# Two token tiles of x, each loaded in two parts of rows on two DMA queues

## The chip, the cores and the metric

The kernel runs on one core of one Trainium2 chip. The metric is the device time of one execution in microseconds. A profile of one execution goes with it: all times of day below are microseconds from the start of that execution's span. TensorE is PE in the profile (PEld for its weight loads), VectorE is DVE, ScalarE is ACT, GpSimd is POOL and SyncE is SP.

## The reference

The input x has 2048 tokens of 512 features in bf16. It is normalised without scale or shift, and two branches run on the result: a diagonal state-space layer (S5) and a SwiGLU feed-forward layer. Both are added to x.

```python
x = A_x
xn = _layernorm(x, axis=-1)
return x + _A_ref(xn, ...) + _B_ref(xn, B_w_gate, B_w_up, B_w_down)
...
g = _silu(x @ w_gate)
u = x @ w_up
return (g * u) @ w_down
...
h = Lam_bar[None, :] * h + Bu[:, t, :]
...
y = 2.0 * jnp.einsum("blp,dp->bld", hseq, Cmat).real + x * Dskip[None, None, :]
```

The hidden width of the feed-forward layer is 1376, the state size 512.

## The kernel before, in words

**Tiling.** The tokens are cut into 16 tiles of 128 and four chunks of 512. The features are cut into four blocks of 128 (index k). The hidden width of 1376 is cut into groups of 512, 512 and 352 columns (`fgroups`, L89). Everything is written out once; the engines run their instructions in the order of the program, and semaphores join them.

**The first chunk is special.** TensorE has nothing to do until tokens arrive, so the first tiles are handled with the tokens as the stationary operand. Tiles 0 and 1 of x are not normalised first. TensorE transposes the raw rows with an identity matrix (`raw_mm`, L233, matmuls at L230), VectorE adds up each row in the meantime (`sum_dve`, L222), and a small matmul takes the mean off the transposed tile in PSUM (`cT_mean`, L238). ScalarE and VectorE copy the result to SBUF (`raw_copy`, L245). Then the products with w_up follow, one feature block k at a time (`row_mm`, L712, matmuls at L487): four matmuls of 512 columns for each k, two tiles by two column groups. The products with w_gate come next, and the scale of the normalisation is put on when ScalarE reads the products (L495, L507). Tiles 2 and 3 are centred or normalised first.

**The loads at the start.** SyncE's queue carries, in this order: tile 0 of x (L123), the four rows of w_up (L117, one for each k, 256 KB each), two rows of w_gate, tile 2 of x (L131), a row of w_gate, tile 3 (L133), the last row of w_gate, the ends of both weights (L113), and tiles 4 to 7 (L141). Tile 1 of x goes on ScalarE's queue (L125), ahead of the load of ScalarE's activation table (L126). A small write of zeros by VectorE into tile 1 (L124) comes before it: the transfer overwrites those bytes and so waits for the write. GpSimd's queue carries three small rows of parameters (L140). A program assigns the transfers of SyncE and ScalarE to eight semaphores in turn, so that one is not issued before the transfer eight places earlier has landed.

**The dummies.** While the first tile is on its way, TensorE multiplies constants (`dummy`, L666, matmuls at L668): four matmuls of 512 columns and then five of 128 (L692 and L693). Their results are not used. They stand ahead of all other work in TensorE's order.

**After that** the chunks follow in a software pipeline: products with the S5 input matrix (L380), gate and up products (L455), the scan on VectorE (L422), the down products (L598) and the S5 output products (L611) accumulate in one PSUM bank for each output tile.

The lines around the change:

```python
120  ident = const.tile([128, 128], BF16, name="ident")
121  make_identity(nc, ident[:])
123  nc.sync.dma_start(out=xall[:, 0, :], in_=x_v[:, 0, :])
124  nc.vector.memset(xall[:, 1, 0:2], 0.0)
125  nc.scalar.dma_start(out=xall[:, 1, :], in_=x_v[:, 1, :])
126  nc.scalar.preload_act_table_set("silu_and_others")
127  for k in range(KD):
128      load_row(nc.sync, wu01, wu_v, k)
...
692  dummy(warm, 4, CW)
693  dummy(warm, 5, 128)
697  raw_mm(0)
```

Of the kernel before, what the change touches and what calls it, by code (L numbers as in the profile page):

```python
# [23 lines left out]
def kernel(  # L24
# [17 lines left out]
    nc = tc.nc  # L42
# [37 lines left out]
    x_v = A_x[0].rearrange("(n p) d -> p n d", p=128)  # L80
# [5 lines left out]
    xall = const.tile([128, NT, D], BF16, name="xall")  # L86
# [33 lines left out]
    ident = const.tile([128, 128], BF16, name="ident")  # L120
    make_identity(nc, ident[:])
    minus_mean = const.tile([128, 128], BF16, name="minus_mean")
    nc.sync.dma_start(out=xall[:, 0, :], in_=x_v[:, 0, :])  # L123
    nc.vector.memset(xall[:, 1, 0:2], 0.0)  # L124
    nc.scalar.dma_start(out=xall[:, 1, :], in_=x_v[:, 1, :])  # L125
    nc.scalar.preload_act_table_set("silu_and_others")  # L126
    for k in range(KD):
        load_row(nc.sync, wu01, wu_v, k)
# [97 lines left out]
    warm = pair[0][0][1]  # L226
# [439 lines left out]
    def dummy(ps, n, cols):  # L666
        for _ in range(n):
            nc.tensor.matmul(ps[:, 0:cols], lhsT=one.to_broadcast([128, 128]), rhs=one.to_broadcast([128, cols]),  # L668
                             start=True, stop=True)
# [20 lines left out]

    G, U = wg_g, wu_g
    dummy(warm, 4, CW)  # L692
    dummy(warm, 5, 128)  # L693
    nc.vector.tensor_scalar(out=minus_mean[:], in0=ident[:], scalar1=-1.0 / D, scalar2=None, op0=ALU.mult)
    for i in range(2):
        sum_dve(i, sums[:, i:i + 1])
# [208 lines left out]
```

## Time and profile before

| | |
|---|---|
| time, median of 3 runs | 178.27 us (178.15 to 178.41) |
| span of the profiled execution, first to last instruction | 175.8 us |
| median over the span | 2.5 us more |
| TensorE busy | 171.4 us |
| VectorE busy | 156.9 us |
| ScalarE busy | 102.0 us |
| GpSimd busy | 28.1 us |
| read from and written to HBM | 8.03 and 5.24 MB |

The profile records one execution. Its own time is known by its span; what lies before the first and after the last instruction is not in it, and the medians of the runs stand 2.5 us above the span. Several views of the trace are used. The chain that ended last is followed back from the last instruction, at each step to what released it. The timeline lists instructions in order of time, merged where one follows another of the same line. A view by window gives each engine's busy time, the granted TensorE clock, the share of the DMA engines' time that was used and GB/s. "Us to landing" is the time from the issue of a transfer to the semaphore that tells that all of it has arrived. An engine name with a q (SPq, ACTq) is that engine's sequencer, which issues transfers.

### The profile page before, as it was taken

The numbers are of one execution on the slowest core, as the hardware profiler recorded it, in microseconds if no ns is written. First come the engines' busy times: TensorE is split into PE (matmuls) and PEld (weight loads), VectorE is DVE, ScalarE is ACT, GpSimd is POOL, SyncE is SP. The second block draws the span as 40 slices with busy tenths as digits, with TensorE's granted clock in tenths as the row PEclk, the third lists the DMA queues.
The fourth block names the chain that finished last, engine by engine and source line by source line (L and its number), as shares of the span: only waits on it lengthen the run. The fifth ranks groups of instructions, "written<-read, shape, count | busy, mean of one in ns | idle before, by whom it ended". The sixth has DMA issues, their size and how long they took to land.

```text
span 175.8 us, 2365 instructions
## 1 busy us (share of the span) xinstructions
PE 171.4 (97%) x847; PEld 82.6 (47%) x863; DVE 156.9 (89%) x259; ACT 102.0 (58%) x188; POOL 28.1 (16%) x39
## 2 busy tenths in 40 slices
PE   8999999999999999999999999999999999999993
PEld 4544446464444444446444444446444444444542
DVE  3776999999999999999999999999999998699542
ACT  3379498793997685236598660024666653990100
POOL 5244110032000000044300000025000000522500
PEclk9999999999999999999999999999999999999999
DMA  5998929999999300047016000007200000696921
GB/s 184 344 350 83 245 48 205 285 191 300 161 218 306 112 4 0 0 38 82 2 34 119 0 0 0 0 0 87 36 15 17 0 4 0 87 175 96 117 66 60
DMA packets 34043, 17.88 MB, mean 102 GB/s; under 512 B 24896, under 2 KB 32928, under 8 KB 33984
## 3 DMA queue, kind: packets, MB, share of 16 engines
q1 hardware_dynamic: 30288, 14.22, 34.1%
q0 software_dynamic: 3456, 3.28, 14.4%
q10 hardware_dynamic: 288, 0.23, 0.4%
q8 instruction: 7, 0.11, 0.3%
q14 instruction: 4, 0.03, 0.1%
HBM read 8.03 MB, written 5.24 MB: 75 GB/s over the span
## 4 chain that ended last, share of the span: by engine, by line
PE 96%; DMA 1%; issue 1%; DVE 0%
PE ps L455 29%; PE ps L598 22%; PE ps L611 16%; PE ps L380 16%; PE ps L487 8%; PE ps L541 3%; PE ps L771 2%; DMA xall<-in_A_x_dram 1%; PE ps L230 1%; PE ps L238 0%; DVE xall L614 0%; PE ps L271 0%
## 5 line engine op out<-in xcount | busy, mean ns | idle before, releaser
L598 PE MATMUL ps<-wd_sb,guT 128*128 128x512 bf16 (+4 forms) x184 | 38.7, 366 | 0.2
L422 DVE TENSOR_TENSOR_SCAN g<-r_t,car,u 128x512 bf16<-128x512 f32 x24 | 29.1, 1264 | 0.0
L611 PE MATMUL ps<-CF,wt 128*128 128x512 bf16 (+2 forms) x134 | 28.4, 366 | 0.1
L380 PE MATMUL ps<-xnT,BT 128*128 128x512 bf16 x125 | 28.1, 379 | 0.2
L598 PEld LDWEIGHTS <-guT 128*128 128x128 bf16 (+1 forms) x187 | 17.9, 98 | 20.5
L455 PE MATMUL ps<-xnT,wu 128*128 128x512 bf16 x95 | 24.6, 379 | 0.2
L455 PE MATMUL ps<-xnT,wg 128*128 128x512 bf16 x91 | 23.9, 379 | 0.1
L618 POOL DMA_DIRECT2D out_dram<-res x12 | 10.5, 1043 | 77.3 <-ACT res L617 72.1
L469 ACT ACTIVATE guT<-ps 128x512 bf16<-128x512 f32 x30 | 18.3, 609 | 4.8 <-PE ps L455 4.5
L470 ACT CAST u<-ps 128x512 bf16<-128x512 f32 x30 | 17.9, 596 | 4.6 <-PE ps L455 4.5
L382 ACT CAST u<-ps 128x512 bf16<-128x512 f32 x32 | 17.5, 597 | 4.8 <-PE ps L380 3.3
L611 PEld LDWEIGHTS <-wt 128*128 128x128 bf16 x136 | 13.0, 98 | 14.7
L380 PEld LDWEIGHTS <-BT 128*128 128x128 bf16 x128 | 12.5, 98 | 14.8
L617 ACT CAST res<-ps 128x512 bf16<-128x512 f32 x12 | 6.8, 583 | 21.0 <-PE ps L611 21.0
L572 ACT ACTIVATE xr<-xall,nb,rstd 128x512 bf16<-128x512 bf16 x16 | 11.8, 805 | 9.1 <-DVE xall L580 4.9
L455 PEld LDWEIGHTS <-wu 128*128 128x128 bf16 x96 | 9.4, 98 | 11.3
L455 PEld LDWEIGHTS <-wg 128*128 128x128 bf16 x96 | 9.3, 98 | 10.6
L192 POOL TENSOR_TENSOR rstd<-ve,neg_half 128x1 f32<-128x1 f32 (+1 forms) x7 | 7.6, 1079 | 29.4 <-DVE ve L191 29.0
L455 PE MATMUL ps<-xnT,w_end 128*128 128x512 bf16 x48 | 10.9, 379 | 0.0
L182 DVE BATCH_NORM_STATS2 stats<-xall 128x6 f32<-128x512 bf16 x16 | 10.8, 675 | 0.0
L474 DVE TENSOR_TENSOR guT<-guT,u 128x1024 bf16<-128x1024 bf16 x15 | 10.0, 675 | 0.0
L390 DVE TENSOR_TENSOR pm<-g,c 128x2048 bf16<-128x2048 bf16 x8 | 9.8, 1220 | 0.1
(120 smaller groups left out, 207.8 us busy)
## 6 DMA issues: line engine op xcount, KB each, us to landing
out_dram<-in_A_x_dram SPq DMA_DIRECT2D x3, 512.0 KB, 5.3
out_dram<-res POOLq DMA_DIRECT2D x12, 128.0 KB, 3.1
out_dram<-xall POOLq DMA_DIRECT2D x3, 512.0 KB, 6.0
wd_sb<-in_B_w_down_dram SPq DMA_DIRECT2D x1, 1280.0 KB, 8.2
wu<-in_B_w_up_dram SPq DMA_DIRECT2D x4, 256.0 KB, 3.8
wg<-in_B_w_gate_dram SPq DMA_DIRECT2D x4, 256.0 KB, 4.8
xall<-in_A_x_dram SPq DMA_DIRECT2D x1, 1024.0 KB, 7.0
xall<-in_A_x_dram SPq DMA_DIRECT2D x1, 512.0 KB, 6.1
```

The lines of the kernel that those rows point to most:

```text
L182: nc.vector.bn_stats(out=stats[:, n, 0, :], in_=xall[:, n, :])
L380: nc.tensor.matmul(ps[:] if c else by_k(ps[:]), lhsT=BT[:, part, k, q * 128:(q + 1) * 128], rhs=xnT[:, c, k, :] if c else xnT0[:, k], star ...
L382: nc.scalar.copy(out=u_tiles[c][:, part, q, :], in_=ps[:])
L422: V.tensor_tensor_scan(out=g()[:, part, q, :], data0=r_t[:, q:q + 1].to_broadcast([128, CW]), data1=u_tiles[c][:, part, q, :], initial=ini ...
L455: nc.tensor.matmul(ps[:fs, lo:hi], lhsT=wslice(groups, fi, k), rhs=xnT[:, c, k, lo:hi], start=(k == 0), stop=(k == KD - 1))
L469: nc.scalar.activation(out=guT[:fs, fi, :], in_=psg[:fs], func=ACT.Silu)
L470: nc.scalar.copy(out=u_pair[c][:fs, fi % 2, :], in_=psu[:fs])
L487: nc.tensor.matmul(ps[:, 0:(b - a) * 128], lhsT=tokens(i, k), rhs=groups[gi][:, k, 0:(b - a) * 128], start=(k == 0), stop=(k == KD - 1))
L572: nc.scalar.activation(out=box["xr"][:], in_=xall[:, n, :], func=ACT.Identity, scale=rstd[:, n:n + 1], bias=nb[:, n:n + 1])
L598: nc.tensor.matmul(o[:], lhsT=gu_tiles[c][:fsz[fi], fi, i * 128:(i + 1) * 128], rhs=wd_sb[:fsz[fi], fi, lo:hi], start=(fi == 0), stop=False)
L611: nc.tensor.matmul(o[:], lhsT=w_tiles[c][:, part, q, i * 128:(i + 1) * 128], rhs=CF[:, part, q, lo:hi], start=False, stop=(part == 1 and q ...
L618: nc.gpsimd.dma_start(out=out_v[:, n, lo:hi], in_=res[:, lo:hi], accum_op=ALU.add)
```

## The change

Tiles 0 and 1 of x are each loaded in two parts: rows 0 to 87 by SyncE's queue, rows 88 to 127 by ScalarE's. Both queues take tile 0 first and tile 1 after it. The write of zeros is gone, and nothing holds a transfer. The dummies are four of 512 columns and three of 128.

```diff
-    nc.sync.dma_start(out=xall[:, 0, :], in_=x_v[:, 0, :])
-    nc.vector.memset(xall[:, 1, 0:2], 0.0)
-    nc.scalar.dma_start(out=xall[:, 1, :], in_=x_v[:, 1, :])
+    XS = 88
+    for i in range(2):
+        nc.sync.dma_start(out=xall[0:XS, i, :], in_=x_v[0:XS, i, :])
+        nc.scalar.dma_start(out=xall[XS:128, i, :], in_=x_v[XS:128, i, :])
     nc.scalar.preload_act_table_set("silu_and_others")
...
     dummy(warm, 4, CW)
-    dummy(warm, 5, 128)
+    dummy(warm, 3, 128)
```

## The prediction

> **What bounds the kernel now.** Start with the page's first part and its chain of work that ended last.
>
> ```profile
> PE 171.4 (97%) x847; PEld 82.6 (47%) x863; DVE 156.9 (89%) x259; ACT 102.0 (58%) x188; POOL 28.1 (16%) x39
> ...
> PE 96%; DMA 1%; issue 1%; DVE 0%
> ```
>
> TensorE is busy 97% of the span and is 96% of the chain. Only the start of the span, before TensorE has data, can be shortened by moving loads. The chain in order of time (start, length, what) shows that start.
>
> ```profile
> 0.68 0.06 issue
> 0.74 2.48 DMA xall<-in_A_x_dram
> 3.22 0.04 issue
> 3.27 0.61 PE ps L230 x4
> 3.87 0.26 PE ps L238 x2
> 4.13 0.43 PE ps L230 x4
> 4.56 0.58 PE ps L238 x4
> 5.14 4.32 PE ps L487 x20
> ```
>
> Token tile 0 of x is issued at 0.74 and lands at 0.74 + 2.48 = 3.22 us. From there on the chain is TensorE alone: transposes of tile 0 (L230), mean corrections (L238), the same for tile 1, then the up products (L487). Tile 1's landing is not in the chain. The timeline of the first microseconds shows what lies beside it (start, length, engine, line).
>
> ```profile
> 0.74 0.39 SPq L123 DMA_DIRECT2D xall<-in_A_x_dram  x1
> ...
> 0.81 0.06 DVE L124 MEMSET xall<- 128x1 uint32 x1 [0.81 <-PEq L889]
> ...
> 0.90 0.38 ACTq L125 DMA_DIRECT2D xall<-in_A_x_dram  x1
> ...
> 1.19 1.84 SPq L117 DMA_DIRECT2D wu<-in_B_w_up_dram  x4
> ...
> 1.31 1.28 ACT L126 ACT_TABLE_LOAD   x1 [1.31 <-DVE e_t L162]
> ...
> 2.02 0.15 PEld L668 LDWEIGHTS <-const-bfloat16-1.0 128*128 128x128 bf16 x1 [0.28 <-issue]
> 2.44 0.47 PEld L668 LDWEIGHTS <-const-bfloat16-1.0 128*128 128x128 bf16 x4 [0.28 <-issue]
> ...
> 3.24 0.42 DVE L222 SCALAR_TENSOR_TENSOR xnT<-xall 128x256 bf16<-128x256 bf16 x1 [1.70 <-DMA xall<-in_A_x_dram]
> 3.26 0.34 PEld L230 LDWEIGHTS <-xall 128*128 128x128 bf16 x4 [0.35 <-DMA xall<-in_A_x_dram]
> ...
> 3.73 0.13 PEld L238 LDWEIGHTS <-sums 128*128 128x128 bf16 x2
> ...
> 3.82 0.47 PEld L230 LDWEIGHTS <-xall 128*128 128x128 bf16 x4
> 4.25 0.47 PEld L238 LDWEIGHTS <-sums 128*128 128x128 bf16 x4
> ...
> 4.98 3.62 PE L487 MATMUL ps<-wu,CF 128*128 128x512 bf16 x16
> ```
>
> Read the pace out of the starts. A 512-column dummy took 2.44 - 2.02 = 0.42 us from start to start; a 128-column one (0.47 - 0.15)/3 = 0.107. The transposes at 3.82 and the corrections at 4.25 still go at 0.107. The sixteen up products go at (3.62 - 0.38)/15 = 0.216 for 512 columns. So TensorE runs at half rate into the corrections and at full rate from the first up product on; I put the change at 4.95 us. This matters most below: **work brought forward into the time before 4.95 is worth half.**
>
> **The change, part by part.** (1) Tile 0 comes as 88 rows on SyncE's queue and 40 on ScalarE's, at once, and tile 1 behind it in the same way. The packet counts of the DMA view show how it went before; q1 is SyncE's queue and q10 ScalarE's. In order, the stretches are 1.70 to 2.13, 2.13 to 2.48 and 2.48 to 2.90.
>
> ```profile
> q1 hardware_dynamic: 62, 0.06, 41.4%
> ```
>
> ```profile
> q10 hardware_dynamic: 59, 0.06, 48.4%
> q1 hardware_dynamic: 52, 0.04, 34.7%
> ```
>
> ```profile
> DMA packets 120, 0.14 MB, mean 322 GB/s; under 512 B 16, under 2 KB 92, under 8 KB 120
> ...
> q1 hardware_dynamic: 58, 0.08, 70.7%
> q10 hardware_dynamic: 62, 0.05, 35.8%
> ```
>
> Tile 0 is 128 packets of 1 KB. 62 went by 2.13, by SyncE's queue alone. Then tile 1 came in on ScalarE's queue and took 59 of the next 111 packets, so that tile 0 was not through at 2.48: of q1's 58 later packets, 120 - 92 = 28 are 2 KB packets of the weights, and about 30 are tile 0's remainder with its completion writes. The hold on tile 1 (the memset, worth 0.90 - 0.74 = 0.16 us) did not keep it out of tile 0's way. Two rows by window give the rates with one queue and with two (last column, GB/s; the 1.00 is the granted TensorE clock, which does not show the half rate).
>
> ```profile
> 1.70:2.10 0.40, 0.40 (x3) 0.12 (x2) 0.00 (x0) 0.40 (x1) 0.32 (x1) 1.00 0.40 141
> 2.10:2.50 0.40, 0.40 (x3) 0.12 (x2) 0.00 (x0) 0.40 (x1) 0.40 (x2) 1.00 0.88 305
> ```
>
> After the change both queues carry tile 0 from the start. Lower end of its landing: the 66 packets left at 2.13, alone at the rate of both queues (111 packets in 0.35 us), would be through at 2.13 + 0.21 = 2.34 instead of somewhere in 2.48 to 2.90; with the late end of that stretch, 0.5 us earlier, a landing at 2.7. Upper end: nothing gained, 3.22. Tile 1 is now issued one issue later (0.74 + 0.45 = 1.19) and meets tile 0's tail again, so I take **2.9**, near the middle. Each reader of x now waits for two transfers; I add 0.02 us for a second wait. Tile 0 is ready 0.30 us earlier.
>
> Tile 1 must follow by the time its transposes come up, 3.82 - 3.22 = 0.60 us after tile 0, at 3.5. Before, it landed at 0.90 + 2.6 = 3.5.
>
> ```profile
> xall<-in_A_x_dram ACTq DMA_DIRECT2D x1, 128.0 KB, 2.6
> ```
>
> Issued at 1.19 with the same 2.6 us it would land at 3.8, 0.3 us late, and the whole gain would be spent on waiting for it; but it too is now carried by both queues, and if it gains the 0.3 us that I give tile 0, it lands at 3.5 and is just in time. I take no stall; the other end is no gain at all, which is inside rival B's time. ScalarE issues two transfers of 0.38 us and begins its table load (1.28 us) at about 1.55 instead of 1.31; it ends at 2.8, and ScalarE's first copy comes after 3.7. That is hidden.
>
> (2) The memset goes: 0.06 us of VectorE, which waits for tile 0 from 0.94 to 3.24 anyway. Nothing.
>
> (3) Two dummies of 128 columns fewer: 2 x 0.107 = 0.21 us. The last dummy ended TensorE's queue at 2.97; now it is 2.76. With tile 0 at 2.92, five dummies would have held it up by 0.05 us. That is all this edit is worth, unless the idle time touches the pace (below).
>
> (4) What is moved: every weight load on SyncE goes one issue (0.45 us) later. The landings of the four up rows, issued at 1.19, 1.65, 2.12 and 2.60, are in two answers of the source view (min/median/max; the first for rows 0 and 1, the second for rows 2 and 3).
>
> ```profile
> DMA to landing us min/median/max: 3.0/3.3/3.6
> ```
>
> ```profile
> DMA to landing us min/median/max: 4.0/4.2/4.4
> ```
>
> They land at 4.2, 5.3, 6.1 and 7.0. They are due at 4.98 and then every 4 x 0.216 = 0.86 us: 5.84, 6.71, 7.57, so 0.5 to 0.8 us of slack. The bytes before them are the same, so the least delay is nothing, and a full issue, 0.45 us, gives 4.65, 5.75, 6.55, 7.45: still ahead of the old due times, at most level with the new ones (0.30 and later 0.15 earlier). I take no stall and keep 0.15 us for the range, all that is gained. The later loads (gate rows, tiles 2 and 3) wait for the landings of transfers eight places earlier in the order of issue, as before.
>
> **The sum.** Tile 0 at 2.92 instead of 3.22 brings the first up product from 4.98 to 4.68. The transposes before it run at the old pace. From 4.68 to 4.95 TensorE does 0.27/0.427 = 0.63 of an up product, at full rate worth 0.14 us; the last 0.03 counts whole. So 0.15 to 0.17 us less: the span goes from 175.8 to 175.65. The three times around it have a median of 178.27, 2.5 us above the span; I keep that offset: **178.1 us**. All that follows is TensorE-bound and moves with it. Here 0.2% is 0.36 us, about what a measurement of this kernel can tell from no change.
>
> The Trainium skill, TensorE: Matmul & The Clock Gate (Part 1, the clock gate), says that full rate comes after a busy window of about 3.4 us of a free-running counter, so by time and not by the number of matmuls. The trace agrees as far as one profile can: the rate changes 4.2 us after the first dummy (0.78), and by that rule bringing work forward gains half, as in the sum above.
>
> **The rivals.** A: **the whole 0.3 to 0.5 us is gained.** If the pace follows the work instead of the clock, closing TensorE's idle time between 2.97 and 3.26 brings full rate forward too. Then the gain is the landing's own: 0.30 (177.97) to 0.52 us (177.75). For it: the rate changes 0.2 us before the first up product, so a link to the work is not excluded; against it: 0.29 us of idle time is little beside the 4.2 us from the first dummy to the change.
>
> B: **the split does nothing.** If SyncE's and ScalarE's transfers only interleave, tile 0 lands at 3.2 as before; two dummies fewer only lengthen an idle time, and the time is 178.3. For it: both queues end within 0.3 us of each other today. Against it: 141 and 305 GB/s with one queue and with two. The Trainium skill, DMA: Bandwidth & Descriptors (Rules for kernel authors), takes this side: two transfers to disjoint partition halves serialize, "Use one 128-partition transfer". By that rule the time would be B's; the doubled rate in the windows speaks against it at this early moment.
>
> C: **the weights come late.** One issue (0.45 us) plus the time of one more tile at 305 GB/s (131 KB, 0.43 us) as upper end puts up row 1 at 6.17, 0.33 us after its old due time, and rows 2 and 3 by 0.3: 178.6. It decides once the delay passes the old slack of 0.55 us. The Trainium skill, DMA: Bandwidth & Descriptors (Why a DMA increments its semaphore by 16 and not by 1), says that a transfer runs on the largest number of engines up to 16 that divides its rows: 88 rows on 11, 40 on 10, the lowest-numbered ones. No trace here shows it; it would leave five engines without x and give ten of them half as much again, a reason for C.
>
> D, the slow side: **TensorE reaches full rate later.** If tile 0 still lands near 3.2, TensorE idles from 2.76, 0.5 us instead of 0.3. Should that break the warm-up, each microsecond of half rate beyond 4.95 costs 0.5 us; a whole further stretch like the one from 0.78 to 4.95 costs 2.1 us: up to 180.4. Point of decision: idle time over the 0.29 us that is known to do no harm. The trace has no such gap to price.
>
> **Chances.** Forecast 0.40 (its own range 178.0 to 178.25), A 0.25 (0.20 of it below 177.91), B 0.12, C 0.13 (0.08 above 178.63), D 0.10. So faster by over 0.2%: 0.20; within: 0.40 + 0.05 + 0.12 + 0.05 = 0.62; slower: 0.08 + 0.10 = 0.18. The range 177.6 to 178.9 takes in A's and C's ends and leaves out most of D and a little beyond both.
>
> **What would show it.** Tile 0's landing in the chain at 2.8 to 3.0 confirms step 1; 3.2 means B. The first L487 at 4.65 to 4.75, with its first start-to-start near 0.43, confirms the half rate; at 0.216 at once, it is A. A wait of PE or PEld on wu between 4.6 and 8.4 is C. Spacing of 0.43 beyond 5 us is D.

## The result and the profile after

The change made the kernel slower: 179.56 us median of 9 executions (178.59 to 181.22) against 178.18 us (177.88 to 178.89, 9 executions of the kernel before on the same chip). The ratio is 1.009, 95% interval 1.0066 to 1.0113; the medians lie 1.38 us apart. Three of the nine executions lie above 180.8 us and the other six at 178.59 to 179.65. The profiled execution of the changed kernel is one of the three: 180.86 us, span 178.7 us. In the kernel after, every line from L126 on stands one lower than before (L487 is L488).

The page's first part and its chain of work that ended last, after:

```profile
PE 174.1 (97%) x861; PEld 82.7 (46%) x861; DVE 156.9 (88%) x258; ACT 103.8 (58%) x188; POOL 28.1 (16%) x39
...
PE 96%; DMA 1%; ACT 0%; DVE 0%; issue 0%
```

TensorE is busy 2.7 us longer, though it has two dummies less to do. Of that, 1.85 us lie ahead of the first product with w_gate (9.41 us busy instead of 7.56): time went into slower matmuls there. The rest can't be read as work, because the trace of the kernel before lacks some matmul records (847 beside 863 weight loads). The chain of the first 12 us (start, length, what) and TensorE's timeline of the same stretch:

```profile
0.74 2.50 DMA xall<-in_A_x_dram
3.25 0.14 issue
3.38 0.58 PE ps L231 x4
...
4.67 0.44 PE ps L239 x3
5.11 0.02 issue
5.13 0.44 ACT CF L246 x2
5.58 0.03 issue
5.61 6.33 PE ps L488 x20
```

```profile
0.78 2.18 PE L669 MATMUL ps<-const-bfloat16-1.0 128*128 128x512 bf16 x7 [0.78 <-PEq L890]
3.38 0.58 PE L231 MATMUL ps<-ident,xall 128*128 128x128 bf16 x4 [0.42 <-DMA xall<-in_A_x_dram]
...
5.61 5.47 PE L488 MATMUL ps<-wu,CF 128*128 128x512 bf16 x16 [0.30 <-ACT CF L246]
10.91 1.03 PE L488 MATMUL ps<-wg,CF 128*128 128x512 bf16 x4
```

The last row is the first gate product. In the kernel before it is this one:

```profile
8.43 1.03 PE L487 MATMUL ps<-wg,CF 128*128 128x512 bf16 x4
```

Tile 0 lands at 0.74 + 2.50 = 3.24 us, no earlier than before (3.22). The first up product starts at 5.61 instead of 4.98, and the sixteen take 5.47 us instead of 3.62. In the starts of the single matmuls they come every 0.427 us until 9.4 us and every 0.216 us from there on: half rate lasts 4.4 us longer than before. The row names ScalarE's copy (L246) as what the first up product waited for, but the semaphore of up row 0 comes at 5.56 in the trace, last of all that it needs. The weights are late, and the view by source line says by how much (the four up rows, issued at 1.2 to 2.6 us before and 1.6 to 2.9 after; first before, then after):

```profile
DMA to landing us min/median/max: 3.0/3.8/4.4
```

```profile
L117 SPq DMA_DIRECT2D wu<-in_B_w_up_dram x4: 359/430/432, 1.6 to 2.9; - x4
...
DMA to landing us min/median/max: 4.0/5.3/5.6
```

They are issued 0.3 to 0.4 us later and take 1.0 to 1.6 us longer. The up rows land at 5.56, 7.18, 7.83 and 8.50, before at 4.19, 5.29, 6.17 and 7.00. The windows 3 to 4 and 4 to 5 us (last two columns: DMA share and GB/s), before and after:

```profile
3.00:4.00 1.00, 0.92 (x9) 0.61 (x8) 0.76 (x4) 0.00 (x0) 0.55 (x2) 1.00 1.02 343
4.00:5.00 1.00, 1.00 (x11) 0.89 (x9) 0.36 (x3) 0.27 (x1) 0.00 (x0) 1.00 1.05 296
```

```profile
3.00:4.00 1.00, 0.62 (x6) 0.50 (x7) 0.49 (x3) 0.00 (x0) 0.54 (x2) 1.00 0.88 210
4.00:5.00 1.00, 1.00 (x10) 0.94 (x9) 0.58 (x3) 0.27 (x1) 0.00 (x0) 1.00 0.72 214
```

In this pair of profiles a third of the bytes is missing while the weights should come, and the DMA engines have idle shares that they did not have before. The experiments below say how far that holds. In the first window four more profiles with the loads of before (e2, e12, e14, e15) have 258 to 329 GB/s and the splits of both tiles with five dummies or more 210 to 261, so there the split does carry less. In the second window they have 163 to 271 and 295 to 358: that shortage belongs to the profiled execution. Last, the end. SyncE's timeline has the last stores (start of the first, time until the last is issued), before and after:

```profile
168.07 5.75 SPq L615 DMA_DIRECT2D out_dram<-xall  x4
```

```profile
170.55 5.75 SPq L616 DMA_DIRECT2D out_dram<-xall  x4
```

The view of waits has what SyncE's final line waits for (total, times, longest), before and after:

```profile
SPq L900 <- DMA out_dram<-xall: 0.5, 1, 0.5
```

```profile
SPq L901 <- DMA out_dram<-xall: 1.0, 2, 0.5
```

The last store is issued by 173.82 before and by 176.30 after. From there to the end of the span (175.85 and 178.70) it is 2.03 us before and 2.40 after; after, the final line waits a second time for such a store. The program ends with SyncE waiting for the eight DMA semaphores in a fixed order. In the trace's semaphore records, the last store's semaphore is the last of the row before. After it, with 42 transfers instead of 40 on the two queues, the turn of the eight has moved on by two: the last store has the second semaphore of the row, and when it lands at 177.41 the rest of the row is still worked off, one wait per 0.062 us, until 177.79.

So the 2.85 us of these two spans divide into 0.63 until the first up product, 1.85 from there to the first gate product (8.43 to 10.91, less the 0.63), and 0.37 at the end. From the first gate product to the last store's issue both take 165.39 us. This compares a late execution of the changed kernel with a quick one of the kernel before. Of the 1.38 us between the medians the end is the same 0.37; the two parts at the start are not the median's.

### The profile page after: what moved, and what is told of

Same layout as the page of the kernel before. It is cut to its first block, busy times and chain, and to the rows that moved or that the text cites. A ratio compares the mean times of both kernels' runs of the same rounds, so it can differ in the third digit from the quotient of the medians.

```text
span 178.7 us, 2383 instructions
## 1 busy us (share of the span) xinstructions
PE 174.1 (97%) x861; PEld 82.7 (46%) x861; DVE 156.9 (88%) x258; ACT 103.8 (58%) x188; POOL 28.1 (16%) x39
## 4 chain that ended last, share of the span: by engine, by line
PE 96%; DMA 1%; ACT 0%; DVE 0%; issue 0%
PE ps L456 29%; PE ps L599 21%; PE ps L612 15%; PE ps L381 15%; PE ps L488 9%; PE ps L542 3%; PE ps L772 2%; DMA xall<-in_A_x_dram 1%; PE ps L231 1%; PE ps L239 0%; ACT CF L246 0%; DVE xall L615 0%; PE ps L272 0%
## 5 line engine op out<-in xcount | busy, mean ns | idle before, releaser
L456 PE MATMUL ps<-xnT,wg 128*128 128x512 bf16 x96 | 24.6, 379 | 0.0
```

The source lines that it names most:

```text
L456: nc.tensor.matmul(ps[:fs, lo:hi], lhsT=wslice(groups, fi, k), rhs=xnT[:, c, k, lo:hi], start=(k == 0), stop=(k == KD - 1))
```

## The experiments

Theories named in the expectations: W, rows cut 88 and 40 load the DMA engines unevenly and delay the weights; Q, two queues with four issues do so; N, each transfer ahead of the weights costs; S, it is the bytes on the second queue; P, the wait for the later part of a tile; G, too much idle time of TensorE lets one period of its clock pass at half rate; L, the row of waits at the end. Each was run beside the kernel before on the same chip. All times in us. "Onset" is when the spacing of TensorE's matmuls goes from 0.427 to 0.216 in the profiled execution.

**The parts alone: the dummies, the hold.**

```diff
e2_3dummies, from before:    -    dummy(warm, 5, 128)
                             +    dummy(warm, 3, 128)
e14_8dummies, from before:   +    dummy(warm, 8, 128)
e12_no_hold, from before:    -    nc.vector.memset(xall[:, 1, 0:2], 0.0)
```

> The loads of the kernel before, with three short dummies instead of five: the idle time ahead of tile 0 grows from 0.3 to 0.5 us. G says 179 or more. W and Q say no more than 0.2 us from before, 178.0 to 178.4, with the first up row landing at 4.2.

> The kernel before with eight short dummies instead of five, so that TensorE hardly idles ahead of tile 0. It is the one version the runs point to that could beat both. G says that no window of the kernel before fails, so there is nothing to win: ratio 0.998 to 1.001. Below 0.998 would mean that the 0.3 us of idle time costs something in the kernel before as well.

> The kernel before without the write of zeros alone: tile 1 goes out on ScalarE's queue at 0.74 instead of 0.90. N and S both expect nothing measurable, 178.1 to 178.5, with tile 0 landing up to 0.2 us later and the first up row at 4.0 to 4.3.

Measured: e2 178.31 (two of 12 executions at 179.97 and 205.47, the others up to 179.34), ratio 1.0005 [0.9982, 1.0029]; e14 178.36, 0.999 [0.9977, 1.0003]; e12 178.51, 1.0007 [0.9992, 1.0022]. Neither the dummies nor the hold alone make a difference that these intervals show. (In e2's profile tile 0 lands at 3.00, and TensorE idles for less than 0.1 us before it, so e2 hardly tests a longer idle time.) Their profiles show something else. They have the weight loads of the kernel before, but not its landings; e12, then e2 (same view as above):

```profile
DMA to landing us min/median/max: 3.0/4.5/4.8
```

```profile
DMA to landing us min/median/max: 2.9/4.5/4.7
```

In e2, e12, e14 and e15 (below) up row 1 lands at 6.02 to 6.36, in the profile of before at 5.29. That profile had caught a quick execution: its span is 175.85 us, while the median span of the kernel before in the five later sessions is 176.25 to 176.5.

**The split with other numbers of dummies.**

```diff
e1_split_5dummies, from after:  -    dummy(warm, 3, 128)
                                +    dummy(warm, 5, 128)
e7_filled, from after:          +    dummy(warm, 8, 128)
    and before the up products: +    dummy(warm, 5, 128)
```

> The split loads of the change with all five short dummies kept. Theory W (88 and 40 rows spread x unevenly over the DMA engines, so the weights come late) and theory Q (four issues on two queues at once make the weights late, however the rows are spread) both say: first up row still lands at about 5.5 us instead of 4.2, time within 0.4 us of the changed kernel, 179.2 to 179.9. Theory G (the two dummies fewer open an idle gap that delays TensorE's full rate) says: back near the kernel before, 178.0 to 178.5.

> The changed kernel with its idle times on TensorE filled: eight short dummies instead of three ahead of tile 0 and five more ahead of the first up product, 13 instead of 3. They add only useless work. G (full rate comes late because TensorE's idle times make a window of its activity fail) says: no execution over 180.2 us (the changed kernel had 3 of 9), median 178.8 to 179.2, below the changed kernel's 179.56. W and Q alone say: no faster than the changed kernel, 179.5 to 179.9.

Measured: e1 179.06 (178.59 to 179.93, 12 executions), ratio 1.0037 [1.0023, 1.005]; e7 179.19 (179.08 to 179.32, 6), 1.0055 [1.0039, 1.0072]. With TensorE kept busy no execution goes above 180, which speaks for G in the executions above 180.8; a loss of 0.4 to 0.6% stays. e1 lies between what was expected of G and of W and Q. TensorE's timeline of e1 shows the weights:

```profile
5.12 1.89 PE L488 MATMUL ps<-wu,CF 128*128 128x512 bf16 x8 [0.50 <-DMA wu<-in_B_w_up_dram]
7.38 1.89 PE L488 MATMUL ps<-wu,CF 128*128 128x512 bf16 x8 [0.37 <-DMA wu<-in_B_w_up_dram]
```

Two waits on wu, 0.87 us together, and full rate already from 4.01: the gain of an early clock is spent waiting for weights. That alone does not tell the split from the others: e4 (below), which loses nothing, waits 0.79 us for wu in two rows of the same kind.

**Other cuts of the rows.**

```diff
e3_rows96_32, from after:   -    XS = 88
                            +    XS = 96
e5_rows96_5dummies: XS = 96 and dummy(warm, 5, 128)
e9_rows112_16:      XS = 112 and dummy(warm, 5, 128)
```

> The change with the cut at row 96 instead of 88: the same four issues on the same queues, but 96 and 32 are both multiples of 16. W says the weights come back: first up row by 4.7 us, time 177.9 to 178.5. Q says nothing changes: first up row at 5.4 or later, 179.2 to 179.9. G says 179 or more too, since the dummies are as few, but with the weights on time.

> The split at row 96 with all five short dummies. Against the split at 88 with five (ratio 1.0037) it changes the spread of rows alone. W (the uneven spread of 88 and 40 rows makes the weights late) says the loss goes: ratio 1.001 or less. Q (two queues with two issues each, whatever the rows) says 1.003 to 1.005. G (the clock: two dummies fewer let a window of TensorE's activity fail in some executions) says that the executions over 180.2 us, 3 of 12 at row 96 with three dummies, are gone.

> Both tiles split at row 112 (112 rows on SyncE, 16 on ScalarE), five short dummies: four transfers ahead of the first up row, but only 32 KB on the second queue. Theory N (each transfer put ahead of the weights costs them time, however few its rows): the first up row at 4.9 or later, 178.8 to 179.2, as with 88 and 96 rows. Theory S (the bytes that share the engines from two queues cost it): first up row within 0.2 us of the 4.6 of two whole tiles on SyncE, 178.2 to 178.5.

Measured: e3 179.12 (178.6 to 181.2, 12; three above 180.3), 1.0058 [1.0031, 1.0086]; e5 178.98, 1.0048 [1.0031, 1.0066]; e9 179.27, 1.0051 [1.0037, 1.0066]. W falls: 96 and 32 rows cost as much as 88 and 40. S falls by the time: 16 rows on the second queue cost as much as 40. But e9's first up row lands at 4.59, where S had it; in its profile, its slowest execution, TensorE waits 0.29 us for tile 1 instead. The late executions come back in e3, with three dummies. Over the splits of both tiles, 6 of 33 executions with three dummies lie above 180.2 (the changed kernel, e3, e16) and none of 38 with five (e1, e5, e9, e17; e8 below stands apart). Five dummies do not rule them out: one of 138 executions of the kernel before beside these runs took 180.53, and one of 12 of e18 (below) 180.45.

**Parts of the split, and the weights ahead of it.**

All three have five short dummies and no hold. e6 and e10 split tile 0 alone; e8 is the split of the change with the first up row between SyncE's two parts.

```diff
e6_tile0_split, from after:
-        nc.sync.dma_start(out=xall[0:XS, 1, :], in_=x_v[0:XS, 1, :])
-        nc.scalar.dma_start(out=xall[XS:128, 1, :], in_=x_v[XS:128, 1, :])
+    nc.scalar.dma_start(out=xall[:, 1, :], in_=x_v[:, 1, :])
e10_tile0_112_16, from e6:
-    XS = 88
+    XS = 112
-    nc.scalar.dma_start(out=xall[:, 1, :], in_=x_v[:, 1, :])
+    nc.sync.dma_start(out=xall[:, 1, :], in_=x_v[:, 1, :])
e8_row0_ahead, from after:
+    load_row(nc.sync, wu01, wu_v, 0)      (the loop over the rows then starts at 1)
     nc.sync.dma_start(out=xall[0:XS, 1, :], in_=x_v[0:XS, 1, :])
```

> Only tile 0 is split (88 and 40 rows); tile 1 comes whole on ScalarE's queue behind the 40 rows, five short dummies. SyncE then issues the first up row at 1.2 us, as before the change. If it is SyncE's one issue more that makes the weights late: first up row at 4.0 to 4.5 us, time 177.9 to 178.5. If sharing the two queues from the start is what slows the transfers: first up row at 4.8 or later, 178.9 or more. W says something between, since half of the uneven transfers are left: 178.5 to 178.9.

> Tile 0 split at row 112, tile 1 whole behind it on SyncE, five short dummies: three transfers ahead of the first up row. N: between two (178.3) and four (179.0), 178.5 to 178.8. S: 178.2 to 178.5.

> Both tiles split at 88, five short dummies, but SyncE issues the first up row between its part of tile 0 and its part of tile 1. If the later issue of the weights is the loss, the first up row lands by 4.5 us and the time is 178.0 to 178.6, though tile 1 comes up to 0.5 us later. If the split itself slows all transfers (W or Q), 178.9 or more.

Measured: e6 179.92, half of 12 executions at 178.54 to 179.19 and half at 180.66 to 181.2, ratio 1.0095 [1.0059, 1.0132]; e10 178.69, 1.0032 [1.0018, 1.0046]; e8 181.05, all four at 180.78 to 181.55, 1.0162 [1.014, 1.0183]. e8 was meant to bring the weights back and instead makes tile 1 late. TensorE's timeline of e8, then of e6:

```profile
5.00 0.59 PE L233 MATMUL ps<-ident,xall 128*128 128x128 bf16 x4 [0.95 <-DMA xall<-in_A_x_dram]
...
6.02 5.34 PE L490 MATMUL ps<-wu,CF 128*128 128x512 bf16 x16
```

```profile
5.22 0.61 PE L231 MATMUL ps<-ident,xall 128*128 128x128 bf16 x4 [1.33 <-DMA xall<-in_A_x_dram]
...
6.26 4.66 PE L488 MATMUL ps<-wu,CF 128*128 128x512 bf16 x16
```

An idle TensorE of 0.95 us before 5 us, and every execution of e8 is of the late kind; onset is 9.5 in e8 and 8.36 in e6. These are the clearest runs for G: what costs is not the idle time alone but also the period at half rate that follows. Sixteen up products at 0.216 would take 3.46 us; in e6 it is 4.50 us to the first gate product (6.26 to 10.76) and in e8 5.18 (6.02 to 11.20), so the half rate costs 1.0 and 1.7 us here, and the rest is the later start. The two halves of e6's executions, about 2 us apart, differ in both: with tile 1 as late as in its profile, full rate throughout would still mean some 179.6 us, and the quick half lies below that. That the idle time delays the rate is argued from these cases; no run changes the idle time alone.

**Both tiles on one queue, and transfers for nothing.**

```diff
e4_whole_on_sync, from before:
-    nc.vector.memset(xall[:, 1, 0:2], 0.0)
-    nc.scalar.dma_start(out=xall[:, 1, :], in_=x_v[:, 1, :])
+    nc.sync.dma_start(out=xall[:, 1, :], in_=x_v[:, 1, :])
e11_both_in_one, from before:
+    nc.sync.dma_start(out=xall[:, 0:2, :], in_=x_v[:, 0:2, :])
e13_whole_plus_two, from e4:
+    extra = const.tile([16, 2, D], BF16, name="extra")
+    for i in range(2):
+        nc.scalar.dma_start(out=extra[:, i, :], in_=x_v[0:16, i, :])
```

> Tiles 0 and 1 whole, one after the other on SyncE's queue, no hold, five dummies: the weights are issued one issue (0.45 us) later, as in the change, from one queue and spread evenly. If the later issue makes the weights late (part of Q), the first up row lands at 5 us or later and the time is 178.8 or more. W says it lands at 4.2 to 4.65 and the time stays within 0.3 us of 178.2.

> Tiles 0 and 1 in one transfer of 256 KB on SyncE's queue, no hold, five short dummies: one transfer ahead of the first up row, issued at 1.2 again. Tile 0 is complete only with tile 1, at 3.2 to 3.5. N: first up row at 4.2 or earlier, time 178.0 to 178.4. S has no quarrel with that; it says the same. If the idle time ahead of tile 0 grows to 0.5 us, theory G expects at most a single execution over 179.3.

> Both tiles whole on SyncE (178.31, ratio 0.9999), and beside them two transfers of 16 rows on ScalarE's queue into a buffer that nobody reads. Everything that TensorE and VectorE wait for is as in the whole-tile kernel; only two small transfers more stand ahead of the weights. N says: the loss of the split at row 112, ratio 1.004 to 1.006, 179.0 to 179.3. If the loss is that a tile is complete only when the later of its two parts has landed (theory P), ratio 1.001 or less, 178.2 to 178.5.

Measured: e4 178.31, 0.9999 [0.9981, 1.0017]; e11 178.62, 1.0011 [0.9999, 1.0024]; e13 179.13, 1.0034 [1.0019, 1.005]. In e13 nobody waits for the added parts, and it costs as much as e1; but e18 (below) shows that e13's loss is of another kind, so this does not dispose of P. The traces do: in e1, e5 and e7 TensorE's rows show no wait for a part of x, and they lose time all the same. By number of transfers ahead of the weights, 1, 2, 3 and 4 gave 1.0011, 0.9999, 1.0032 (e10; e6, with its late tile 1, apart) and 1.0034 to 1.0051 (with five dummies): a step between two and three, where N expects a slope. e10 and e13 are also kernels in which the span from the first gate product to the end is 0.4 us longer; in e4 and e11 it is not. That led to L.

**The end alone, and the end taken back.** Small loads into a tile that nobody reads, on SyncE's queue at about 55 to 61 us, when it is idle. They only turn the eight semaphores on.

```diff
+    mid = const.tile([16, 2, 64], BF16, name="mid")
+    for i in range(2):
+        nc.sync.dma_start(out=mid[:, i, :], in_=x_v[0:16, i, 0:64])
e15_before_plus2:         these two, in the kernel before
e16_after_plus6:          six of them, in the changed kernel
e17_split5_plus6:         six of them, in e1
e18_whole_plus_two_plus6: six of them, in e13
```

> The kernel before with two small loads (16 rows of 64 columns into a tile that nobody reads) on SyncE's queue in the middle, at about 54 us, when that queue is idle. The start is untouched. Theory L (about 0.4 us of the loss is the row of waits at the end, because two more transfers on the two queues put the last store's semaphore earlier in that row): the first gate product keeps its time, the span from there to the end is 167.8 instead of 167.4 us, the time 178.6 to 178.8, ratio about 1.002. If the loss is all at the start (N, W, G): no change, 178.3, ratio 1.000.

> The changed kernel with six such small loads in the middle, so that with the two of the change it has eight transfers more than before and the last store has its old semaphore again. The start is that of the changed kernel. Theory L: the span from the first gate product on is 167.4 us again, and the time is 0.4 us under the 179.56 of the changed kernel: about 179.15, ratio 1.005, with up to a third of the executions still above 180 from the late full rate. If the number of transfers does nothing at the end: 179.5, ratio 1.007 to 1.009.

> The split with five short dummies and the six small loads in the middle. Theory L: what is left is the start alone, 178.6, ratio 1.001 to 1.002 instead of 1.0037. If the number of transfers does nothing at the end: ratio 1.003 to 1.005, 179.0.

> Both tiles whole on SyncE's queue, the two small unused loads on ScalarE's queue at the start, and the six small loads in the middle. Theory L: the two loads at the start cost what they delay the weights, 0.0 to 0.2 us, and the ratio falls from 1.0034 to 1.001. Theory N (each transfer issued ahead of the weights costs): ratio still 1.003.

Measured, 12 executions each: e15 178.82, 1.0023 [1.0009, 1.0038]; e16 178.75 (178.5 to 179.57), 1.002 [1.0004, 1.0036]; e17 179.03, 1.0034 [1.0018, 1.0049]; e18 178.37, 1.0004 [0.9982, 1.0026]. SyncE's last stores in e15, then in e16:

```profile
168.72 5.75 SPq L615 DMA_DIRECT2D out_dram<-xall  x4
```

```profile
169.59 5.75 SPq L616 DMA_DIRECT2D out_dram<-xall  x4
```

And the waits of SyncE's final line, in e15 and in e16:

```profile
SPq L903 <- DMA out_dram<-xall: 1.0, 2, 0.5
```

```profile
SPq L904 <- DMA out_dram<-xall: 0.5, 1, 0.5
```

The second wait comes to the kernel before and goes from the changed kernel. From the last issue to the end it is 2.39 us in e15 (176.86 - 174.47) and 2.03 in e16 (177.37 - 175.34); 2.04 in e17 and 2.02 in e18, after 2.41 in e1 and 2.39 in e13. So L is shown in both directions: two loads far from the start cost the kernel before 0.42 us, and six more take the end of the changed kernel, of e1 and of e13 back. The place in the row gives the size: with the last store's semaphore in first place (41 transfers: e6, e10) it is 2.45 to 2.46 us, in second place (42) 2.39 to 2.41, in seventh (39: e11) 2.09, in eighth (40 or 48) 2.01 to 2.04. So the step between two and three transfers above is the end's. With the end taken back, e13's loss is gone (N falls for these small loads), and the changed kernel's goes from 1.009 to 1.002; that is more than the 0.37 us of the end (0.2%). e17 missed: its end is back, its time is not, 179.03 after 179.06. Its profile has the weights late again:

```profile
5.02 1.02 PE L488 MATMUL ps<-wu,CF 128*128 128x512 bf16 x4 [0.40 <-ACT CF L246]
6.51 2.75 PE L488 MATMUL ps<-wu,CF 128*128 128x512 bf16 x12 [0.47 <-DMA wu<-in_B_w_up_dram]
```

e16 was expected at 179.15 and came 0.4 lower, with none of 12 executions above 180 where the changed kernel had three of 9. Its start is the changed kernel's own, so the share of late executions is not settled by these counts, nor is the rest of e16's gain.

What is left at the start can be read from one number per profile, when the first gate product starts, since what follows takes the same time but for the end (167.40 to 167.48 us, with the late end 167.78 to 167.85; e16 alone has another 0.5 us between them):

| kernels | up row 0 lands | up row 1 lands | first gate product |
|---|---|---|---|
| loads of before (before, e2, e12, e14, e15) | 4.03 to 4.19 | 5.29 to 6.36 | 8.43, 9.02, 8.68, 8.82, 9.09 |
| whole tiles, loads in another order (e4, e11, e13, e18) | 4.18 to 5.44 | 5.37 to 6.21 | 9.16, 9.13, 9.12, 9.20 |
| both tiles split, five dummies or more (e1, e5, e7, e9, e17) | 4.59 to 5.20 | 5.84 to 6.47 | 9.10, 8.86, 9.05, 9.45, 9.10 |
| both tiles split, three dummies (after, e3, e16) | 5.02 to 5.56 | 5.69 to 7.18 | 10.91, 9.26, 9.46 |

The means for the loads of before and for the splits with five dummies are 8.81 and 9.11. But e4, e11 and e18, whose times are within 0.11% of the kernel before, start as late as the splits, so single profiles do not show a loss at the start. The record also has the span of every execution, to 0.1 us. If what follows the first gate product takes the same time in each, the median spans put it later than in the kernel before beside them by 0.2 us in e1 and e5, 0.3 in e7 and e9 and 0.4 in e17, and by -0.1 to 0.1 in e4, e10, e11, e13 and e18 (with three dummies 0.3 in e3 and 0.0 in e16): an estimate, but one that goes with the times.

The same record shows a third part of the loss, which no view of the profile has. Time less span has a median of 2.03 to 2.06 us in the kernel before (138 executions in five sessions) and of 2.03 to 2.09 in the ten experiments with a whole tile 0 or 1. In all nine kernels with both tiles split (the changed kernel, e1, e3, e5, e7, e8, e9, e16, e17) it is 2.16 to 2.32. So 0.1 to 0.26 us of the split's cost lie ahead of the first instruction or behind the last. What takes them is open. The three parts add up: 0.2 at the start, 0.37 at the end and 0.2 outside make some 0.7 us in e1, where 0.68 was measured; 0.4 and 0.26 make 0.66 in e17, which has its end back, where 0.63 was measured.

Why the weights behind four split transfers come later is not settled: not the cut of the rows (e5, e9), and not the number of transfers alone (e18 gets its row 0 at 4.39, in the same order of issue as e13, whose profile shows 5.44).

## Why the prediction was wrong, point by point

The forecast was 178.1 us with a range up to 178.9; the time is 179.56. **What bounds the kernel** held: TensorE is 96% of the chain after as before, and only the start and the end moved.

**Step 1, the landing of tile 0: its reason failed.** In the profile after, tile 0 lands at 3.24, not 2.9: rival B's landing, without B's time. One profile does not settle the landing: with the loads of before it lands at 3.00 to 3.40 (before, e2, e12, e14, e15), and with the very parts of the change at 2.82 to 3.00 in e1, e7 and e17 and at 3.24 in e16. These scatter as widely as the gain that was forecast. What did fail is the reason given, that two queues move tile 0 at twice the rate of one. The step took the 62 packets that SyncE's queue had sent by 2.13 as given and let two queues send the rest at the later rate. The DMA view of 1.70 to 2.13, after:

```profile
DMA packets 26, 0.03 MB, mean 62 GB/s; under 512 B 0, under 2 KB 26, under 8 KB 26
...
q10 hardware_dynamic: 21, 0.02, 45.6%
q1 hardware_dynamic: 5, 0.01, 5.3%
```

Here two queues together sent 26 packets where one had sent 62. In the other profiles this stretch scatters (1.70 to 2.10 us: 20 to 141 GB/s with the loads of before, 136 to 205 in e1, e5, e7, e9 and e17), so the 62 were no given. The issues themselves grew, and the timeline shows them; two issues each, on ScalarE and on SyncE:

```profile
0.74 0.92 ACTq L126 DMA_DIRECT2D xall<-in_A_x_dram  x2
...
0.74 0.79 SPq L125 DMA_DIRECT2D xall<-in_A_x_dram  x2
```

The first ones take 0.60 and 0.43 us, where the whole tiles took 0.38 and 0.39; the second ones take 0.29 and 0.30. The rate of two queues at 2.1 to 2.5 us was that of a later moment, not of a second queue. e4 shows it, with both tiles on SyncE's queue alone:

```profile
1.70:2.10 0.40, 0.40 (x3) 0.12 (x2) 0.00 (x0) 0.32 (x1) 0.32 (x1) 1.00 0.80 118
2.10:2.50 0.40, 0.40 (x3) 0.12 (x2) 0.00 (x0) 0.00 (x0) 0.40 (x2) 1.00 0.97 274
```

The rate more than doubles without a second queue (all 122 packets of the second row are q1's), and tile 0 lands at 2.88 (2.93 and 2.98 in e18 and e13, also whole). The rule that two transfers to disjoint partition halves serialize (the Trainium skill, DMA: Bandwidth & Descriptors, Rules for kernel authors), which the prediction set aside, agrees with the landing in this profile, 3.24 against 3.22 us; over the other profiles no run here decides it.

**Steps 2 and 3**, the hold and the dummies, held when alone (e12, e2). With the split, three dummies leave TensorE idle for 0.42 us before tile 0 by its row, and late executions were frequent only in splits with three, or where tile 1 came late (e6, e8).

**Step 4, "I take no stall", failed.** Its upper end for a weight row's delay was one issue, 0.45 us in that step; rival C's was 0.88. Row 0 came 0.8 to 1.4 us later in the 88 and 40 splits. The later issue is not what costs: e4 issues its first up row at 1.65, as late as the split, and loses nothing. And the slack of 0.5 to 0.8 us was read from one quick execution: in four other profiles with the same loads row 1 lands 0.7 to 1.1 us later than there, behind the time when the prediction had it due.

**The sum's "all that follows is TensorE-bound and moves with it" failed at the end**: 167.41 us from the first gate product on before, 167.79 after. No term of the sum had the end in it, and no rival. The offset between span and time, 2.5 us, was off too, and it was not constant: 2.05 us in the kernel before and 2.16 in the changed one. So the profile of before stood some 0.3 us below the median of 178.18, and another 0.1 us of the loss is in no term.

**The rivals.** B had the landing of this profile, C the late weights, D the late clock. In the profiled execution the loss is the two last together with the end, and of these only the end is shown by runs that change it alone. D's point of decision, idle time over 0.29 us, is not a threshold: TensorE idled 0.42 us before tile 0 in the changed kernel and 0.41 in e16's same start, with late executions in one and none in the other; e11, with five dummies, idles 0.40 us there and has none in 12. D's price was right in size: a whole further stretch at half rate was put at 2.1 us, and cost 1.85 here. What was wrong is that C and D were taken as alternatives: weights that are late are also idle time of TensorE (0.30 us before the first up product), and may raise D.

The Trainium skill, TensorE: Matmul & The Clock Gate (Part 1, the clock gate), has the rate follow a free-running window of about 3.4 us. The runs agree in the main: onset lies at 3.5 to 6.6 us wherever TensorE is kept busy and at 8.4 to 9.5 in the profiles of the late kind (after, e6, e8), about one window later. The earliest, in e14, is only 2.7 us after the first dummy, so a window need not be busy from end to end; how much idle time spoils one, no run here shows.

## What to carry to other kernels

Before a load is cut into more transfers, count what stands behind it on its queue and what its number does elsewhere: here two transfers more moved the last store to an earlier place in the program's final row of waits, 0.4 us far from the edit. Take slack and landings from several profiles of kernels with the same loads, not from one, and put each execution's time beside its span: a part of a loss can lie outside the span. Where a clock seems to need a stretch of busy time, a short wait at the start may cost the whole stretch, so look at the spread of the executions and not only at the median.

## What the runs showed of the hardware

The end of the program costs by the place of the last store's semaphore: 2.01 to 2.04 us from the last issue where it is the last of eight, 2.39 to 2.41 where it is the second, 0.062 us for each wait left. In the split, 88 rows come with eleven landing signals and 40 with ten in the trace's semaphore records, whole tiles with sixteen; the rule that a transfer uses the largest number of engines that divides its rows (the Trainium skill, DMA: Bandwidth & Descriptors, Why a DMA increments its semaphore by 16 and not by 1) fits these counts, but cutting at 96 did not win the time back.
